# Second product of the first tile half in float32, half in float16 parts, and magnitudes and soft-max high parts of two batches on ScalarE

## The chip, the core and the metric

The kernel runs on one core of a Trainium2 chip. Five engines work side by side, each through its own queue in order: TensorE (PE in the profile; its weight loads are PEld), VectorE (DVE), ScalarE (ACT), GpSimd (POOL) and SyncE (SP), which issues the DMAs here. The metric is the device time of one execution in microseconds (us); less is better.

## The reference

Attention with a sliding window of 128 and a linear bias, then an MLP with Gelu, over 8 batches of 8 heads, 576 positions and 64 per head (4608 tokens, model width 512, inner width 2048):

```python
scores = scale * np.matmul(q, k.transpose(0, 1, 3, 2))
mask = (rel >= 0) & (rel < window)
scores = np.where(mask, scores + bias[None], -1000000000.0)
attn = softmax(scores)
x = concat_heads(np.matmul(attn, v))        # 4608 x 512
h = x @ w_in                                # 512 -> 2048
g = 0.5 * h * (1.0 + erf(h * inv_sqrt2))
out = g @ w_out                             # 2048 -> 512
```

All inputs and the output are float32.

## The kernel before, in words

**Precision.** A float32 matrix is mostly carried as two float16 parts: a high part (the scaled value rounded) and a low part (the scaled value less the high part, line 145). A product is then three float16 matmuls: high by high, high by low, low by high. The scales are powers of two taken from the largest magnitude. Batch 0 of attention (`EXACT = 1`) and the second product of the first tile are done in float32 instead (lines 389 and 619), for which no parts are needed.

**Tiles and stages.** The MLP goes over 9 tiles of 512 tokens. A tile's first product (`mlp_in`, L584) has 16 chunks of 128 inner columns; each is 12 float16 matmuls into one PSUM bank of tag "mm" (four banks), and ScalarE's Gelu empties it (L597 for tile 0, L600 for the others). For tile 0, Gelu writes float32 `g` at once. For the others it writes float32, GpSimd makes the high part (L601) and VectorE the low one. The second product (`mlp_out`) adds all 16 chunks into one bank for each of four blocks of 128 tokens; tile 0 takes the float32 weights `zo` (L619), the others the weight parts `wo` (L622).

**Attention.** One unit is two heads of one batch; a batch has four. `scores` (L399) fills banks of tag "att", VectorE scales them and adds the bias (L421), `softmax` takes the maximum (L491, VectorE), the exponential (L494, ScalarE), the reciprocal of the sum (L498), the high part `e_main` (L500, GpSimd) and the low part (VectorE, L145); a transposing DMA on SP's queue turns them into `et`, and `weigh` (L540) multiplies by v. ScalarE and VectorE cut the result into the parts of `x`, the MLP's input. While tile t is in the MLP, batch t + 1 goes through attention, at steps written out by hand. Tile t takes part of its tokens from batch t and batch t + 1 begins inside it, so a tile needs `weigh` of all four units of batch t before its first product can end.

**q, k and v.** `split_qk` takes the largest magnitude of q and of k (`absmax`, L213, VectorE), spreads it over partitions, and writes the high parts (L356, ScalarE) and the low ones (VectorE) to `qbuf` and `kbuf`, which exist once. `stat_v` and `split_v` do the same for v.

**Weights.** `w_in` and `w_out` come in a packed form and are turned into float32 by two operations of ScalarE (L186, L188) and three of VectorE (L191, L192, L195). Four buffers of tag "wo" hold the float32 `w_out`; its parts need a common scale (`weights_out_scale`), and then take the places of the float32 weights one after the other. Two of the eight pairs of parts go to a buffer of tag "ld", which q and k of batch 2 need next, and are copied from there by a DMA (`wo_first`, L278) when the last "wo" buffer is free.

**Order.** The kernel is written with a framework that keeps all dependencies and plans the order of each engine's queue: it takes the order of the text as priorities (`tc.high_priority` raises some) and issues by modelled times. Buffers are given by tag when a free one of the tag is there. So the text after line 680 (the loop over weight pairs `n` with tile 0's first product, then the loop over `m` with its second product and the units of batch 1, then the tiles) is a wish and the trace shows what came of it.

## Time and profile before

| what | value |
|---|---|
| median of 3 runs | 958.84 us (958.63 to 960.74) |
| profiled execution | 957.65 us, span 955.8 us |
| busy share of the span | PE 96%, DVE 66%, ACT 47%, POOL 27% |
| granted TensorE clock, mean | 0.988 |
| tile 0: first product | about 66 to 111 us |
| tile 0: second product, with batch 1's units | 111.4 to 188.1 us |
| tile 1's first matmul | 187.9 us |
| one steady tile (393.5 to 491.6 us) | 98 us |

The profile has one page (busy shares, 40 equal slices of the span with digits for tenths of busy time, the chain of waits that ended last, the costliest groups) and a trace that answers further questions. In a timeline a row is: start, time, engine, line, operation, tiles (written <- read), shape, count, and in brackets how long the engine had been idle before and what released it. In a table by stage a row gives, for each engine, its busy time and its number of instructions.

### The profile page before, as it was taken

How to read it: one execution, taken by the hardware profiler on the slowest of the kernel's cores; microseconds unless marked ns; L12 is line 12 of the kernel's file. 1: busy time of each engine (PE TensorE's matmuls, PEld its weight loads, DVE VectorE, ACT ScalarE, POOL GpSimd, SP SyncE). 2: the span in 40 equal slices, each digit the busy share in tenths (PEclk: the TensorE clock that was granted, in tenths of full speed). 3: DMA queues.
4: the chain of work that ended last, by engine and by line, in shares of the span. 5: the costliest groups of instructions: out<-in, count | busy, mean ns of one | idle time of the engine just before them, and what ended most of it. 6: DMA issues, size and time to landing. Idle time of an engine off the chain costs nothing.

```text
span 955.8 us, 17566 instructions
## 1 busy us (share of the span) xinstructions
PE 920.2 (96%) x7036; PEld 450.0 (47%) x7036; DVE 634.8 (66%) x1254; ACT 449.5 (47%) x957; POOL 253.5 (27%) x516
## 2 busy tenths in 40 slices
PE   6979999899798999999999999999999999999998
PEld 3554444444454445444544445444544454444443
DVE  6899989769886978588767876777566722201200
ACT  5977556344563665256626643664366313101200
POOL 1010004323441533144313530353044312201200
PEclk8999999899999999999999999999999999999999
DMA  9527615762367424713371346245312430000000
GB/s 324 199 96 244 222 50 74 132 188 100 72 135 166 76 51 106 193 32 66 79 193 45 66 95 171 56 79 95 73 28 51 86 81 1 1 23 23 0 12 34
DMA packets 172451, 91.18 MB, mean 95 GB/s; under 512 B 132561, under 2 KB 153169, under 8 KB 172241
## 3 DMA queue, kind: packets, MB, share of 16 engines
q1 hardware_dynamic: 172368, 90.06, 38.3%
q8 instruction: 55, 0.90, 0.4%
q14 instruction: 28, 0.22, 0.1%
HBM read 46.53 MB, written 9.44 MB: 59 GB/s over the span
## 4 chain that ended last, share of the span: by engine, by line
PE 68%; DVE 8%; ACT 4%; DMA 3%; issue 2%; POOL 1%; SPq 0%; POOLq 0%; ACTq 0%; DVEq 0%
PE o L622 31%; PE h L584 29%; PE av L540 4%; PE sc L399 3%; DMA et<-e_main 2%; ACT s L494 2%; DVE e_main L145 2%; DVE s L421 1%; DVE g L145 1%; DVE nmax L491 1%; DVE stq L213 1%; POOL e_main L500 1%; DMA q<-qp 1%; DVE wo L145 1%; DMA v<-vp 1%
## 5 line engine op out<-in xcount | busy, mean ns | idle before, releaser
L584 PE MATMUL h<-x,wi 128*128 128x512 f16 x1728 | 381.8, 379 | 5.0 <-ACT g L600 3.3
L584 PEld LDWEIGHTS <-wi 128*128 128x128 f16 x1728 | 166.2, 98 | 205.8 <-issue 7.3
L622 PE MATMUL o<-wo,g 128*128 128x512 f16 x1152 | 260.2, 380 | 0.0
L622 PEld LDWEIGHTS <-g 128*128 128x128 f16 x1536 | 145.9, 98 | 175.2 <-issue 0.7
L601 POOL TENSOR_SCALAR g<-g,sg 128x512 f16<-128x512 f32 x128 | 104.2, 818 | 286.1 <-ACT g L600 280.4
L494 ACT ACTIVATE s<-s,nmax 128x192 f32<-128x192 f32 x252 | 111.2, 442 | 121.4 <-DVE nmax L491 114.4
L145 DVE SCALAR_TENSOR_TENSOR g<-g,sg,g 128x512 f16<-128x512 f32 x128 | 106.1, 841 | 90.4 <-POOL g L601 90.3
L500 POOL TENSOR_SCALAR e_main<-s,z 128x192 f16<-128x192 f32 x252 | 121.4, 499 | 126.1 <-issue 43.6
L600 ACT ACTIVATE g<-h,gs 128x512 f32<-128x512 f32 x128 | 86.0, 686 | 135.0 <-PE h L584 108.6
L145 DVE SCALAR_TENSOR_TENSOR e_main<-s,z,e_main 128x192 f16<-128x192 f32 x252 | 111.0, 482 | 15.3 <-POOL e_main L500 14.8
L622 PE MATMUL o<-wo_first,g 128*128 128x512 f16 x384 | 88.3, 379 | 0.0
L399 PE MATMUL sc<-kbuf,qbuf 64*64 64x192 f16 (+1 forms) x1656 | 73.3, 261 | 8.5 <-DMA kbuf<-kp 4.6
L421 DVE SCALAR_TENSOR_TENSOR s<-sc,cs,bias_h 128x384 f32<-128x384 f32 x112 | 63.6, 607 | 12.2 <-PE sc L399 12.0
L553 ACT ACTIVATE x<-av,cx 128x448 f16<-128x448 f32 (+6 forms) x52 | 23.8, 475 | 91.7 <-PE av L540 91.5
L491 DVE TENSOR_REDUCE nmax<-s 128x5 f32<-128x960 f32 (+1 forms) x56 | 58.5, 1044 | 2.7 <-DVE s L421 0.5
L619 PE MATMUL o<-zo,g 128*128 128x512 f32 x128 | 58.1, 606 | 0.0
L540 PE MATMUL av<-et,vbuf 128*64 128x128 f16 (+1 forms) x1680 | 46.0, 215 | 11.9 <-DMA et<-e_main 11.1
L426 POOL MEMSET s<- 64x128 f32 (+1 forms) x112 | 19.1, 171 | 135.1 <-DVE s L421 134.5
L630 ACT ACTIVATE ob<-o,so 128x512 f32<-128x512 f32 x16 | 10.8, 677 | 90.8 <-PE o L622 90.7
L399 PEld LDWEIGHTS <-qbuf 64*64 64x64 f16 x1512 | 36.2, 107 | 36.8 <-issue 33.5
L540 PEld LDWEIGHTS <-vbuf 128*64 128x64 f16 x1680 | 43.0, 114 | 22.2 <-issue 18.4
L632 DVE TENSOR_SCALAR ob<-o,so 128x512 f32<-128x512 f32 x16 | 11.9, 744 | 60.0 <-PE o L622 60.0
(129 smaller groups left out, 737.5 us busy)
## 6 DMA issues: line engine op xcount, KB each, us to landing
v<-vp SPq DMA_DIRECT2D x32, 320.0 KB, 5.2
out<-ob SPq DMA_DIRECT2D x36, 256.0 KB, 2.0
raw<-w_in SPq DMA_DIRECT2D x8, 1024.0 KB, 14.2
raw<-w_out SPq DMA_DIRECT2D x8, 1024.0 KB, 5.0
q<-qp SPq DMA_DIRECT2D x7, 1152.0 KB, 6.1
k<-kp SPq DMA_DIRECT2D x7, 1152.0 KB, 6.0
qbuf<-qp SPq DMA_DIRECT2D x4, 288.0 KB, 4.7
kbuf<-kp SPq DMA_DIRECT2D x4, 288.0 KB, 5.0
```

Of the source, the lines that this page charges most:

```text
L145: nc.vector.scalar_tensor_tensor(out=dst, in0=src, scalar=scale, in1=high, op0=ALU.mult, op1=ALU.subtract)
L399: nc.tensor.matmul(ps[bank][o, n, 0:W], a, m, start=(i == 0), stop=(i == len(terms) - 1 and b > 0), skip_group_check=True,)
L421: nc.vector.scalar_tensor_tensor(out=s[:, bank[0] : bank[0] + k, :], in0=ps[bank][:, 0:k, 0:W], scalar=cs, in1=bias.broadcast_to([P, k, W] ...
L491: nc.vector.tensor_reduce(out=nmax[:, r], in_=s[:, r], axis=AX.X, op=ALU.max, negate=True)
L494: nc.scalar.activation(s[:, i, :], s[:, i, :], AF.Exp, bias=nmax[:, i : i + 1], accum_out=z[:, i : i + 1])
L500: nc.gpsimd.tensor_scalar(e[:, i, 0, c], s[:, i], z[:, i : i + 1], 1.0, op0=ALU.mult, op1=ALU.mult)
L540: nc.tensor.matmul(av[r, (j - blocks[0]) * QB : (j - blocks[0] + len(js)) * QB], v32s[b][:, hp, kb, r] if b < EXACT else vbuf[:, vi, hp, k ...
L584: nc.tensor.matmul(ph, wi[n][:, a, cc, k * P : (k + 1) * P], x[:, cc, b, :], start=(i == 0), stop=(i == 3 * NCC - 1),)
L600: nc.scalar.activation(g32, ph, AF.Gelu, scale=gsc[t, n])
L601: nc.gpsimd.tensor_scalar(g[:, r, 0], g32, gsg[t, n], 1.0, op0=ALU.mult, op1=ALU.mult)
L619: nc.tensor.matmul(o, g[:, r, c], zo[n][:, n % 2, k * DM : (k + 1) * DM], start=(fc == 0), stop=(fc == NFC - 1))
L622: nc.tensor.matmul(o, g[:, r, a, c], wo[n][:, b, k, :], start=(fc == 0 and i == 0), stop=(fc == NFC - 1 and i == 2),)
```

## The change

It edits seven things.

1. Tile 0's second product: token blocks 0 and 1 (`WHOLE = 256` tokens) stay in float32; blocks 2 and 3 take three float16 matmuls with parts of `g` and `wo`. Both kinds of `g` share one buffer: 256 columns of float32, and 256 columns seen as two float16 parts.
2. Tile 0's Gelu is split: 256 columns go to `g`, 256 to a float32 buffer `rest` (tag "ob"), from which ScalarE makes the high part and VectorE the low one.
3. The tile's scales are computed with each pair of weights (`weights_in`) instead of chunk by chunk.
4. `split_qk` of batches 1 and 2 takes the sum of magnitudes on ScalarE (`AF.Abs` with an accumulated sum, writing into `qbuf` and `kbuf`) in place of the maximum on VectorE. The sum is a bound of the maximum, so the scale is smaller.
5. The soft-max high parts of batches 1 and 2 are made by ScalarE instead of GpSimd.
6. `stat_v(1)`, `split_qk(1)`, `split_v(1)` and `load_v(2)` move from pair 3 to pair 7, and a small copy makes the statistics wait for the low part of chunk 8 or 5; `stat_v(2)` moves behind the third step of the second product, and `split_qk(2)` waits for the last sum of batch 1's soft-max.
7. The second product's loop: eight steps in float32, then eight in float16 in the order 2 to 7, 0, 1; the first weight parts are made ahead of it, the others during the float32 steps; scores at steps 1 and 4, `weigh` at 5, 8, 11 and 15.

```diff
+WHOLE = 256
...
         inverse(sww[:, r], pww[:, r])
+        tile_scales(0, ns)
...
-    def split_qk(b):
+    def split_qk(b, gate=None):
         q32, k32 = qk32.pop(b)
         stat = small([P, 2], f"stq{b}", 2, tag="stq")
-        absmax(stat[:, 0:1], q32)
-        absmax(stat[:, 1:2], k32)
+        if gate is not None:
+            nc.vector.tensor_copy(stat, gate.broadcast_to([P, 2]))
+        for n, (src, buf) in enumerate(((q32, qbuf), (k32, kbuf[:, :, PAD:]))):
+            if b < 3:
+
+                nc.scalar.activation(buf[:, 0], src, AF.Abs, accum_out=stat[:, n : n + 1])
+            else:
+                absmax(stat[:, n : n + 1], src)
...
+                if st.b < 3:
+                    nc.scalar.activation(e[:, i, 0, c], s[:, i], AF.Copy, scale=z[:, i : i + 1])
+                    continue
                 nc.gpsimd.tensor_scalar(e[:, i, 0, c], s[:, i], z[:, i : i + 1], 1.0, op0=ALU.mult, op1=ALU.mult)
...
         if t == 0:
-            nc.scalar.activation(g[:, r], ph, AF.Gelu, scale=gsc[t, n])
+            nc.scalar.activation(g[:, r, 0:WHOLE], ph[:, 0:WHOLE], AF.Gelu, scale=gsc[t, n])
+            if k == 0:
+                rests[n] = pool.tile([P, 2, TT - WHOLE], F32, tag="ob", name=f"g32_{t}_{n}", bufs=3)
+            rest = rests[n][:, k]
+            nc.scalar.activation(rest, ph[:, WHOLE:TT], AF.Gelu, scale=gsc[t, n])
+            hi, lo = (halves_of(g, r)[:, a] for a in range(2))
+            nc.scalar.activation(hi, rest, AF.Copy, scale=gsg[t, n])
+            low_part(lo, rest, gsg[t, n], hi)
             return
...
+    def halves_of(g, r):
+
+        return g[:, r, WHOLE:TT].bitcast(F16).rearrange("p (a s) -> p a s", a=2)
+
+    def low_of_first(fc):
+
+        return halves_of(g_of[0, fc // 4], fc % 4)[:, 1, 0:1]
...
+        whole = t == 0 and tb * P < WHOLE
...
-        if t == 0:
-            nc.tensor.matmul(o, g[:, r, c], zo[n][:, n % 2, k * DM : (k + 1) * DM], start=(fc == 0), stop=(fc == NFC - 1))
+        if whole:
+            nc.tensor.matmul(o, g[:, r, c], zo[n][:, n % 2, k * DM : (k + 1) * DM], start=(fc == first), stop=(fc == last))
         else:
+            if t == 0:
+                both, c = halves_of(g, r), slice(tb * P - WHOLE, (tb + 1) * P - WHOLE)
+            else:
+                both = g[:, r]
             for i, (a, b) in enumerate(((0, 0), (0, 1), (1, 0))):
                 nc.tensor.matmul(
-                    o, g[:, r, a, c], wo[n][:, b, k, :],
-                    start=(fc == 0 and i == 0), stop=(fc == NFC - 1 and i == 2),
+                    o, both[:, a, c], wo[n][:, b, k, :],
+                    start=(fc == first and i == 0), stop=(fc == last and i == 2),
                 )
...
-            tile_scales(0, [n])
             for k in range(2):
                 mlp_in(0, 2 * n + k)
-        if n == 3:
-            stat_v(1)
-            split_qk(1)
+        weights_out_raw(n)
+        if n == 7:
+            stat_v(1, low_of_first(8))
+            split_qk(1, low_of_first(5))
             split_v(1)
             load_v(2)
-        if n == 5:
-            stat_v(2)
-        weights_out_raw(n)
         fetch(1)
...
-    scores_at, weigh_at, split_at = {1: 2, 3: 3}, {2: 0, 4: 1, 6: 2}, {5: 0, 6: 2, 7: 4}
-    for m in range(NWP):
+    out_scale(0)
+    weights_out_split(0)
...
+    whole = range(WHOLE // P)
+    todo = [(m, whole, 0, NFC - 1) for m in range(NWP)]
+    order = list(range(2, NWP)) + [0, 1]
+    todo += [(m, range(WHOLE // P, NTB), 2 * order[0], 2 * order[-1] + 1) for m in order]
+    scores_at, weigh_at, split_at = {1: 2, 4: 3}, {5: 0, 8: 1, 11: 2, 15: 3}, {1: 2, 3: 4, 5: 6}
+    for n, (m, tbs, first, last) in enumerate(todo):
         for fc in (2 * m, 2 * m + 1):
-            for tb in range(NTB):
-                mlp_out(0, tb, fc)
-        if m in scores_at:
-            all_scores(unit(1, scores_at[m]))
-            softmax(unit(1, scores_at[m]))
-        if m in weigh_at:
-            weigh(unit(1, weigh_at[m]))
-        if m in split_at:
-            weights_out_split(split_at[m])
-    weigh(unit(1, 3))
-    weights_out_split(6)
+            for tb in tbs:
+                mlp_out(0, tb, fc, first, last)
+        if n in split_at:
+            weights_out_split(split_at[n])
+        if n == 2:
+            stat_v(2)
+        if n in scores_at:
+            all_scores(unit(1, scores_at[n]))
+            softmax(unit(1, scores_at[n]))
+        if n in weigh_at:
+            weigh(unit(1, weigh_at[n]))
     load_qk(2)
-    split_qk(2)
+    split_qk(2, unit(1, 3).z[:, NG - 1 : NG])
```

More of the change, by code (lines that the diff above doesn't have):

```diff
@@ L304, in load_v, with stat_v @@
         v32s[b] = v32
-    def stat_v(b):
+    def stat_v(b, gate=None):
         stat = small([P, 1], f"stv{b}", 2, tag="stv")
+        if gate is not None:
+            nc.vector.tensor_copy(stat, gate)
         absmax(stat, v32s[b].rearrange("p h n d -> p (h n d)"))
@@ L343, in load_qk @@
         qk32[b] = (q32.rearrange("p h s -> p (h s)"), k32.rearrange("p h s -> p (h s)"))
-    def split_qk(b):
+    def split_qk(b, gate=None):
         q32, k32 = qk32.pop(b)
         stat = small([P, 2], f"stq{b}", 2, tag="stq")
-        absmax(stat[:, 0:1], q32)
-        absmax(stat[:, 1:2], k32)
+        if gate is not None:
+            nc.vector.tensor_copy(stat, gate.broadcast_to([P, 2]))
[4 more added lines that the diff above has]
+                absmax(stat[:, n : n + 1], src)
         pw, sc = pow2(f"q{b}", stat, 2, 2, b < 2)
@@ L564, in tile_scales @@
         r = slice(ns[0], ns[-1] + 1)
-        big = k > 1
-        gs = small([P, k], f"gs{t}_{ns[0]}", 2, tag=f"gs{int(big)}")
+        gs = small([P, k], f"gs{t}_{ns[0]}", 4 if t == 0 else 2, tag=f"gs{k}")
         nc.vector.tensor_scalar(gs, pww[:, r], pwx[t], 2.0 ** -26, op0=ALU.mult, op1=ALU.mult)
-        if t == 0:
-            for n in ns:
-                gsc[t, n] = gs[:, n - ns[0] : n - ns[0] + 1]
-            return
-        sg = small([P, k], f"sg{t}_{ns[0]}", 2, tag=f"sg{int(big)}")
+        sg = small([P, k], f"sg{t}_{ns[0]}", 4 if t == 0 else 2, tag=f"sg{k}")
         nc.vector.tensor_scalar(sg, sww[:, r], sx[t], 2.0 ** -22, op0=ALU.mult, op1=ALU.mult)
@@ L575, in tile_scales @@
             gsc[t, n], gsg[t, n] = gs[:, n - ns[0] : n - ns[0] + 1], sg[:, n - ns[0] : n - ns[0] + 1]
+    rests = {}
     def mlp_in(t, fc):
@@ L610, in attention_gelu_mlp, with mlp_out @@
     o_ps = {}
-    def mlp_out(t, tb, fc):
+    def mlp_out(t, tb, fc, first=0, last=NFC - 1):
         n, k = divmod(fc, 2)
-        if fc == 0:
+        whole = t == 0 and tb * P < WHOLE
+        if fc == first:
             o_ps[t, tb] = psum.tile([P, DM], F32, tag="mm", name=f"o{t}_{tb}", bufs=4)
@@ L617, in mlp_out @@
         c = slice(tb * P, (tb + 1) * P)
-        if t == 0:
-            nc.tensor.matmul(o, g[:, r, c], zo[n][:, n % 2, k * DM : (k + 1) * DM], start=(fc == 0), stop=(fc == NFC - 1))
-        else:
+        if whole:
+            nc.tensor.matmul(o, g[:, r, c], zo[n][:, n % 2, k * DM : (k + 1) * DM], start=(fc == first), stop=(fc == last))
+        else:
+            if t == 0:
+                both, c = halves_of(g, r), slice(tb * P - WHOLE, (tb + 1) * P - WHOLE)
+            else:
+                both = g[:, r]
             for i, (a, b) in enumerate(((0, 0), (0, 1), (1, 0))):
                 nc.tensor.matmul(
-                    o, g[:, r, a, c], wo[n][:, b, k, :],
-                    start=(fc == 0 and i == 0), stop=(fc == NFC - 1 and i == 2),
+                    o, both[:, a, c], wo[n][:, b, k, :],
+                    start=(fc == first and i == 0), stop=(fc == last and i == 2),
                 )
-        if fc == NFC - 1:
+        if fc == last:
             ob = pool.tile([P, DM], F32, tag="ob", name=f"ob{t}_{tb}", bufs=3)
-            so_t = so[t] if t else 1.0
+            so_t = 1.0 if whole else so[t]
             if tb % 2:
```

## The prediction

> **What bounds the kernel now.** I read the page's busy table first, then the 40 slices, then busy time by stage, then the timelines of PE and DVE in the stages that the change touches.
>
> ```profile
> span 955.8 us, 17566 instructions
> PE 920.2 (96%) x7036; PEld 450.0 (47%) x7036; DVE 634.8 (66%) x1254; ACT 449.5 (47%) x957; POOL 253.5 (27%) x516
> ...
> PE   6979999899798999999999999999999999999998
> ...
> DVE  6899989769886978588767876777566722201200
> ```
>
> PE is busy for 96% of the span, so what can be won is matmul time (920.2 us) or the 35.6 us in which PE is idle. The slices say where the idle time lies: from slice 14 (about 335 us) on PE reads 9 throughout. DVE is high in the first quarter and falls to 5 to 7 later. So the change, which works on the stage from about 60 to 310 us, meets a stretch in which PE and DVE are both near full. The busy time by stage (engines PE, PEld, DVE, ACT, POOL, then granted clock, DMA share, GB/s):
>
> ```profile
> 60.00:190.00 130.00, 122.93 (x826) 62.46 (x823) 120.17 (x214) 73.64 (x140) 22.49 (x56) 0.96 0.57 149
> 190.00:310.00 120.00, 110.32 (x948) 54.73 (x947) 93.19 (x176) 54.02 (x114) 38.95 (x71) 0.99 0.52 131
> 310.00:400.00 90.00, 90.00 (x812) 43.84 (x812) 71.60 (x147) 47.98 (x108) 32.00 (x66) 1.00 0.46 101
> ```
>
> Tile 0 (60 to 190) leaves PE 7.1 us idle and DVE 9.8. Tile 1 (190 to 310) leaves PE 9.7 and DVE 26.8. After that PE has no idle time, so a microsecond by which tile 2 starts earlier is a microsecond of the whole. The chain of waits, which runs on PE in its last 170 us, says the same; its last row is one half of a tile, and it also gives the price of a float16 matmul: 192 in 41.45 us, 0.216 us each.
>
> ```profile
> 910.61 41.45 PE o L622 x192
> ```
>
> **PE work removed.** The timeline of PE, first for the two products of tile 0, then for its end and for the waits of tile 1:
>
> ```profile
> 80.33 31.24 PE L584 MATMUL h<-x,wi 128*128 128x512 f16 x144 [1.24 <-ACT g L597]
> 111.40 20.76 PE L619 MATMUL o<-zo,g 128*128 128x512 f32 x48
> 132.10 1.42 PE L399 MATMUL sc<-kbuf,qbuf 64*64 64x192 f16 x42
> 174.81 1.60 PE L540 MATMUL av<-et,vbuf 128*64 128x128 f16 x66
> 180.82 2.77 PE L540 MATMUL av<-et,vbuf 128*64 128x128 f16 x66 [4.42 <-DMA et<-e_main]
> 183.53 4.55 PE L619 MATMUL o<-zo,g 128*128 128x512 f32 x8
> 187.92 7.93 PE L584 MATMUL h<-x,wi 128*128 128x512 f16 x36
> 195.78 1.60 PE L540 MATMUL av<-et,vbuf 128*64 128x128 f16 x66
> 197.72 2.75 PE L584 MATMUL h<-x,wi 128*128 128x512 f16 x12 [0.35 <-ACT x L553]
> 225.70 0.68 PE L399 MATMUL sc<-kbuf,qbuf 64*64 64x192 f16 x16
> 241.93 0.27 PE L399 MATMUL sc<-kbuf,qbuf 64*64 64x192 f16 x2 [0.58 <-DVE s L421]
> 259.83 2.32 PE L540 MATMUL av<-et,vbuf 128*64 128x128 f16 x54 [4.08 <-DMA et<-e_main]
> 299.52 1.55 PE L540 MATMUL av<-et,vbuf 128*64 128x128 f16 x54 [2.60 <-DMA et<-e_main]
> ```
>
> A float32 product of the second layer is two records of the trace: 16 chunks by 4 token blocks are 64 calls, and L619 has 128 records. So 48 records are 24 products, and 20.76 / 24 = 0.865 us each. Half of the calls, 32, become three float16 matmuls: 3 x 0.216 = 0.648 us. PE loses 32 x (0.865 - 0.648) = 7.0 us. The whole second product falls from 55.4 to 27.7 + 20.7 = 48.4 us. That is certain as work; whether it is time hangs on what else holds the end of tile 0.
>
> **What holds the end of tile 0.** In DVE's timeline batch 1's last soft-max block comes late (the first two rows are for later):
>
> ```profile
> 101.95 2.57 DVE L213 TENSOR_REDUCE stq<-k 128x1 f32<-128x2304 f32 x1
> 165.57 2.46 DVE L145 SCALAR_TENSOR_TENSOR wo<-zo,s,wo 128x1024 f16<-128x1024 f32 x2
> 179.89 1.93 DVE L145 SCALAR_TENSOR_TENSOR e_main<-s,z,e_main 128x192 f16<-128x192 f32 x4
> 185.54 0.69 DVE L632 TENSOR_SCALAR ob<-o 128x512 f32<-128x512 f32 x1 [3.32 <-PE o L619]
> 187.87 1.42 DVE L145 SCALAR_TENSOR_TENSOR e_main<-s,z,e_main 128x192 f16<-128x192 f32 x4
> ```
>
> It ends at 187.87 + 1.42 = 189.3, its transposing DMA lets the last attention product start at 195.78, and only after it is the input of tile 1 whole (197.72). With 48.4 us of second product, PE would have done its work by 111.4 + 48.4 + 8.4 (scores) + 4.8 (three attention products of 1.6) = 173.0, and the 36 matmuls of tile 1 that it can do ahead (36 x 0.216 = 7.8 us) by 181. The 8.4 us stand in the first row of the next fence. DVE, not PE, then sets this end, so DVE's work is summed. Groups of 60 to 190 us (busy us, mean ns of one):
>
> ```profile
> L399 PE MATMUL sc<-kbuf,qbuf 64*64 64x192 f16 x216 | 8.4, 246 | 0.5 <-DVE s L421 0.5
> L213 DVE TENSOR_REDUCE stq<-q 128x1 f32<-128x2304 f32 x2 | 5.1, 2543 | 0.0
> L213 DVE TENSOR_REDUCE stq<-k 128x1 f32<-128x2304 f32 x1 | 2.6, 2570 | 0.0
> L145 DVE SCALAR_TENSOR_TENSOR x<-tail,sx,x 128x256 f16<-128x256 f32 x1 | 0.5, 479 | 0.0
> L145 DVE SCALAR_TENSOR_TENSOR e_main<-s,z,e_main 128x192 f16<-128x192 f32 x36 | 15.7, 480 | 1.0 <-POOL e_main L500 0.8
> ```
>
> - Removed: three maxima over q and k go to ScalarE, 5.1 + 2.6 = 7.7 us.
> - Added: 16 low parts of 128x256, as `x<-tail`, 16 x 0.479 = 7.7 us. The tile scales keep their number (8 instructions before, 4 + 4 after), and the two copies that serve as gates are of 128x1 and 128x2.
> - The low parts of the weights of attention: the four at 179.89 run beside POOL and take 0.48 us each, the four at 187.87 mostly without it, 0.36. Taking POOL off these 36 is worth between 0 and 36 x 0.12 = 4.4 us; I take half, 2.2.
> - The 3.32 us that DVE waits for `o` go, because that product ends some 10 us earlier for PE.
>
> In the Trainium skill, "GPSIMD Engine Reference", section "8. Key points", POOL shares its SBUF interfaces with VectorE and contends with VectorE instructions that have two SBUF inputs, as these low parts have. By that rule the whole 4.4 us would come back and the forecast would be 2.2 us lower; the two rows agree in direction.
>
> So the last soft-max ends 2.2 + 3.3 = 5.5 us earlier, at about 184, and tile 1's input is whole 5.5 us earlier. PE then waits some 9 us there, in place of the 4.42 us at 180.82; what follows such a wait runs slow for a while (66 matmuls in 2.77 us against 1.60, eight float32 records in 4.55 against 8 x 0.432 = 3.46), and I leave that as it is now, 2.3 us.
>
> **ScalarE's new work** lies beside this. Its rows:
>
> ```profile
> 79.59 2.42 ACT L597 ACTIVATE g<-h,gs 128x512 f32<-128x512 f32 x4
> 141.08 0.45 ACT L494 ACTIVATE s<-s,nmax 128x192 f32<-128x192 f32 x1 [2.79 <-DVE nmax L491]
> L512 ACT ACTIVATE x<-tail,sx 128x256 f16<-128x256 f32 x1 | 0.5, 510 | 0.0
> L356 ACT ACTIVATE qbuf<-q,scq 128x2304 f16<-128x2304 f32 x1 | 2.2, 2201 | 0.0
> L186 ACT ACTIVATE zo<-raw 128x1024 f32<-128x1024 f32 x8 | 9.4, 1170 | 14.5 <-DMA raw<-w_out 14.5
> ```
>
> A Gelu of 128x512 (2.42 / 4 = 0.605 us) becomes two Gelus of half the width and a scaled copy. Each of the three lies between the 0.45 of a 128x192 and the 0.51 of the one 128x256; I take 0.48, nearer the row of the same size: 16 x (3 x 0.48 - 0.605) = 13 us. The sums of magnitudes of q and k are 2 x 2.2 for batch 1 and as much for batch 2. The high parts are 36 x 0.45 = 16 us for each of batches 1 and 2. Up to 190 us ScalarE goes from 73.6 to about 73.6 + 13 + 4.4 + 4.4 + 16 = 111 of 130 us. I cost this at nothing on PE, because the first product has four banks of 2.6 us (12 x 0.216) each before a late Gelu stops it, and behind that product ScalarE has 19 us free before 190. If the cover is gone, a Gelu queued behind a conversion that waits for `raw` (14.5 us over eight of them) delays PE; between 0 and 13 us, and DVE's soft-max, which sets the end, would hide most of it. The new gates hold nothing of DVE: counted on from 80.33, where four chunks are done, PE ends chunk 5 at 85.5 and chunk 8 at 93.3, so their low parts are due by about 87 and 95, while k of batch 1 was reduced only at 102. The statistics and loads of v that move behind them are not due before tile 1.
>
> **Tile 1.** Its waits are 0.58 + 4.08 + 2.60 = 7.3 us, all behind scores and soft-max of batch 2, which begin at 225.70, 38 us after tile 1's first matmul (187.92).
>
> ```profile
> 224.21 2.61 DVE L145 SCALAR_TENSOR_TENSOR kbuf<-k,scq,kbuf 128x2304 f16<-128x2304 f32 x1
> L278 SPq DMA_DIRECT2D wo_first<-wo x1: 542/542/542, 192.9 to 192.9; - x1
> ```
>
> They waited for the parts of q and k, done at 226.8; k's buffer is free only after the copy of the first weight parts (issued on SP's queue at 192.9), which needs the last float32 weight buffer. After the change that buffer is read out 27.7 us of float32 products after 111.4, so the copy can go some 25 us earlier and the scores come at their place, 8 chunks or 21 us after the tile's start instead of 38. DVE loses the maximum over k of batch 2 (2.5) and POOL's neighbourhood once more, and has 26.8 us free. I take 5.5 of the 7.3 us as won; bounds 0 and 7.3 + 0.8 (the slow 2.32 against 1.55 behind the wait).
>
> **The sum.** 5.5 + 5.5 = 11.0 us off the profiled execution of 957.65 (span 955.8 and 1.85 around it): 946.65. The median of the runs shown, 958.84, is 1.2 above it: 947.8.
>
> **Rivals.** *PE sets the end of tile 0 after all.* The scores of batch 1 can start earlier than 132 (two maxima, 5.1 us, no longer stand on DVE ahead of them), and if DVE's idle 9.8 us close up, the attention products wait for nothing. Then the 7.0 us of PE work count in full, with 4.42 + 0.35 and the 2.3 slow us, and all 8.1 of tile 1: 22 us. With half of those waits kept, some 15 to 17 us: 942, at best 937. Against: DVE was 92% busy in this stage (120.17 of 130). Chance 0.2.
>
> *DVE gives nothing back.* The order of issue is planned from modelled times, so the text's new order need not come out as written; the gained idle time reappears as other waits on DVE's in-order queue, now behind ScalarE's high parts, and tile 1's waits stay. Only 0 to 4 us remain: 957. Chance 0.2.
>
> *The weight parts end last (slower).* The float16 half needs all eight weight parts in tile 0; before, the last of them were done at 168 and none was used before tile 1's second product. The last pair stands behind batch 1's last soft-max in the text. If its two low parts (2.46 us) run after 184, they end at 186.5; the copy of the first pair waits for the buffer that they read (0.54 to issue, 5.2 to land: 192.2), then 24 matmuls (5.2) and an eviction (0.7): 198.1. Two of the four banks are held so long, so only 18 instead of 36 matmuls of tile 1 are done by then (3.9 us lost). Tile 1 goes on 0.4 + 3.9 = 4.3 us later than now, with its waits as they are: 963; with a few of them won, 959. It decides from the point where the last low part ends later than 182. Against it: DVE's idle 9.8 us leave room for them earlier. Chance 0.15.
>
> **How the numbers follow.** Forecast 0.45 (6 to 14 us won; 944.8 to 952.8), rivals 0.2, 0.2 and 0.15. Changes within 0.2% (1.9 us), about what a measurement of this kernel can tell from none, are taken from the second rival. Faster 0.45 + 0.2 + 0.12 = 0.77, same 0.08, slower 0.15. The range takes in the forecast, nearly all of the first rival and the second, and leaves out the slower one: 937 to 958.5.
>
> **What would show it.** In the changed profile: 64 records of L619's float32 form and 96 more of the float16 one; PE's busy time near 913; the first product of tile 0 without waits for `g`; batch 1's last low part near 184; the scores of batch 2 about 21 us after tile 1's start; no wait of 4 us in tile 1. I am wrong if PE's first product of tile 0 runs later than 113, if PE waits for `wo` in the float16 half, or if DVE's idle time in tile 0 grows.

## The result

The changed kernel takes 954.13 us (median of 5 runs, 952.48 to 956.14) against 958.84 (5 runs, 958.59 to 962.07): ratio 0.9949, 95% interval 0.9925 to 0.9973. That is 4.7 us faster where 11 were forecast. Run again with the experiments, it took 951.66 against 958.65: ratio 0.993 (0.991 to 0.9949). So the change wins 5 to 7 us.

The page of the changed kernel (span; busy time and share of PE, PEld, DVE, ACT, POOL; the slices of PE and DVE):

```profile
span 954.3 us, 17680 instructions
...
PE 920.4 (96%) x7068; PEld 448.8 (47%) x7068; DVE 626.1 (66%) x1270; ACT 493.4 (52%) x1071; POOL 214.5 (22%) x444
...
PE   7979999889999899999999999999999999999998
...
DVE  6799989689786877497768876777566722201200
```

GpSimd lost 39 us, ScalarE gained 44, VectorE lost 9. PE's busy time is that of before (920.2), not the 913 that were forecast. A second profile of each kernel was taken with the experiments: e14 is the change again, with 913.0 us of PE, and e8 is the kernel before again.

**Where the time went.** The stage that the change touches, cut at the end of tile 1's first product. The columns of these tables by stage are the window, its length, then the busy time of PE, PEld, DVE, ACT, POOL, the granted clock, DMA share and GB/s. Before:

```profile
111.40:234.80 123.40, 115.81 (x843) 56.93 (x843) 102.91 (x203) 58.66 (x119) 34.48 (x68) 0.97 0.47 114
234.80:294.30 59.50, 54.59 (x531) 28.28 (x532) 51.72 (x112) 27.18 (x84) 22.93 (x54) 0.97 0.56 115
```

After:

```profile
114.00:237.30 123.30, 113.33 (x913) 56.95 (x914) 108.45 (x241) 88.97 (x196) 16.49 (x36) 0.96 0.50 121
237.30:288.40 51.10, 51.10 (x493) 25.45 (x494) 41.49 (x78) 31.11 (x92) 3.74 (x14) 1.00 0.63 141
```

The first stretch, from tile 0's second product to the end of tile 1's first, is as long as before: PE is busy 2.5 us less in it (38 records of work, scores above all, moved into it from the second) and idle 2.4 us more (10.0 against 7.6). The second stretch, tile 1's second product, is 8.4 us shorter: 3.5 us of its PE work moved ahead, and 4.9 us of idle time are gone. Since work moved across this cut, a cut at one event is clearer: the start of batch 1's last attention product, which the forecast wanted earlier. All numbers are us, from two profiles of each kernel:

| stretch | before | before again (e8) | change | change again (e14) |
|---|---|---|---|---|
| second product's start to the last attention product of batch 1 | 84.4 | 82.9 | 82.9 | 83.8 |
| PE busy and idle in it | 79.0, 5.4 | 79.4, 3.4 | 74.3, 8.5 | 74.6, 9.2 |
| from there to tile 2's start | 98.5 | 98.5 | 91.5 | 90.9 |
| PE busy and idle in it | 91.4, 7.1 | 91.4, 7.1 | 90.1, 1.5 | 90.1, 0.8 |

Up to that event PE has less to do, and waits as much longer. Behind it, in tile 1, 7.0 to 7.6 us are won, nearly all of it idle time. So the whole gain came in tile 1, and nothing came in tile 0, where half of it was forecast.

**Which waits went and which came.** PE's groups in the whole stage (busy us, mean ns of one, then idle time ahead of the group and what ended it). Before:

```profile
L584 PE MATMUL h<-x,wi 128*128 128x512 f16 x194 | 43.2, 379 | 2.2 <-ACT g L600 1.8 <-ACT x L553 0.3
L399 PE MATMUL sc<-kbuf,qbuf 64*64 64x192 f16 x432 | 16.7, 253 | 1.3 <-DVE s L421 1.3
L540 PE MATMUL av<-et,vbuf 128*64 128x128 f16 (+1 forms) x426 | 13.0, 227 | 9.0 <-DMA et<-e_main 8.5 <-DVE e_main L145 0.5
```

After:

```profile
L595 PE MATMUL h<-x,wi 128*128 128x512 f16 x194 | 43.7, 379 | 2.4 <-ACT ob L661 2.1 <-ACT x L567 0.2
L653 PE MATMUL o<-wo_first,g 128*128 128x512 f16 x72 | 17.5, 394 | 2.8 <-DMA wo_first<-wo 2.8
L410 PE MATMUL sc<-kbuf,qbuf 64*64 64x192 f16 x432 | 17.2, 250 | 2.7 <-DVE s L432 1.5 <-ACT kbuf L367 0.6 <-DVE kbuf L146 0.5
L554 PE MATMUL av<-et,vbuf 128*64 128x128 f16 (+1 forms) x426 | 13.4, 231 | 1.9 <-DMA et<-e_main 1.9
```

The attention products wait 7.1 us less. New are the copy of the first weight parts (2.8), an eviction on ScalarE (2.1) and 1.4 more ahead of the scores. PE's timeline after (start, time, ...) shows their places:

```profile
82.97 31.24 PE L595 MATMUL h<-x,wi 128*128 128x512 f16 x144 [1.11 <-ACT g L612]
114.04 13.90 PE L646 MATMUL o<-zo,g 128*128 128x512 f32 x32
...
170.46 0.59 PE L653 MATMUL o<-wo_first,g 128*128 128x512 f16 x1 [2.77 <-DMA wo_first<-wo]
...
172.07 2.77 PE L554 MATMUL av<-et,vbuf 128*64 128x128 f16 x66
175.84 2.77 PE L554 MATMUL av<-et,vbuf 128*64 128x128 f16 x66 [1.00 <-DMA et<-e_main]
178.54 5.85 PE L653 MATMUL o<-wo_first,g 128*128 128x512 f16 x23
184.23 2.75 PE L595 MATMUL h<-x,wi 128*128 128x512 f16 x12
...
191.97 4.04 PE L595 MATMUL h<-x,wi 128*128 128x512 f16 x18 [2.06 <-ACT ob L661]
196.89 1.60 PE L554 MATMUL av<-et,vbuf 128*64 128x128 f16 x66 [0.88 <-DMA et<-e_main]
199.13 0.28 PE L410 MATMUL sc<-kbuf,qbuf 64*64 64x192 f16 x4 [0.64 <-ACT kbuf L367]
...
320.32 4.89 PE L595 MATMUL h<-x,wi 128*128 128x512 f16 x15 [2.42 <-ACT g L618]
```

Tile 1 begins at 184.23, 3.7 us earlier than before, but the last attention product of batch 1, without which its first product can't end, begins at 196.89 (before: 195.78). The last row is a wait in tile 2. It stands in the place of the 2.60 us at 299.52 before, which the forecast counted to tile 1, though tile 2 had begun at 294.16; the second profiles have the same two waits (2.30 and 2.21).

That tile 1 no longer waits has the reason that was forecast. The copy of the first weight parts, which k's buffer had to wait for, was issued at 192.89 before (81.5 us after the second product's start) and is now issued 50.5 us after it:

```profile
164.55 0.54 SPq L280 DMA_DIRECT2D wo_first<-wo  x1
```

VectorE's timeline tells why batch 1's last soft-max is late:

```profile
136.39 2.82 DVE L214 TENSOR_REDUCE stv<-v 128x1 f32<-128x2560 f32 x1 [2.51 <-DMA v<-vp]
139.13 0.16 DVE L508 TENSOR_SCALAR z<-z 128x5 f32<-128x5 f32 x1
...
163.21 1.27 DVE L146 SCALAR_TENSOR_TENSOR wo<-zo,s,wo 128x1024 f16<-128x1024 f32 x1
...
190.00 0.67 DVE L116 COPY quarters<-stq 32x2 f32<-32x2 f32 x4 [3.17 <-ACT kbuf L358]
...
191.63 0.72 DVE L146 SCALAR_TENSOR_TENSOR e_main<-s,z,e_main 128x192 f16<-128x192 f32 x2
```

And ScalarE's, with one row of SyncE's queue:

```profile
172.89 1.84 ACT L512 ACTIVATE e_main<-s,z 128x192 f16<-128x192 f32 x5 [2.02 <-DMA et<-e_main]
...
176.30 7.38 SPq L517 DMA_TRANSPOSE et<-e_main  x2
...
183.91 1.84 ACT L512 ACTIVATE e_main<-s,z 128x192 f16<-128x192 f32 x5 [2.32 <-DMA et<-e_main]
185.66 2.11 ACT L358 ACTIVATE qbuf<-q 128x2304 f16<-128x2304 f32 x1
...
187.76 2.11 ACT L358 ACTIVATE kbuf<-k 128x2304 f16<-128x2304 f32 x1
...
189.87 1.48 ACT L512 ACTIVATE e_main<-s,z 128x192 f16<-128x192 f32 x4
191.25 0.67 ACT L661 ACTIVATE ob<-o,so 128x512 f32<-128x512 f32 x1
```

The maximum over v of batch 2 stops VectorE's queue for 2.51 us until v has landed, and stands there for 2.82, ahead of a soft-max of batch 1 (L508). The weight part that frees the buffer for the copy comes at 163.21. At the end the two passes over q and k of batch 2 stand on ScalarE ahead of the last four high parts and an eviction, and VectorE's step on their result (190.00) stands ahead of the last four low parts. One more link is in these rows: `e_main`, which holds the parts of a unit's soft-max, exists once, so the high parts of the next unit wait until the transposing DMAs have read it, 2.02 and 2.32 us here (4.3 together in both profiles of the change; before, GpSimd waited 4.1 us so). The last low part ends at 192.35, 78.3 us after the second product's start (78.6 in the second profile); before it was 189.29, 77.9 after (76.4 in the second). That is the step on which the forecast was built.

### The profile page after: what moved, and what is told of

Its sections match the earlier page's. It is cut to its first block, busy times and chain, and to the rows that moved or that the text cites. A ratio compares the mean times of both kernels' runs of the same rounds, so it can differ in the third digit from the quotient of the medians.

```text
span 954.3 us, 17680 instructions
## 1 busy us (share of the span) xinstructions
PE 920.4 (96%) x7068; PEld 448.8 (47%) x7068; DVE 626.1 (66%) x1270; ACT 493.4 (52%) x1071; POOL 214.5 (22%) x444
## 4 chain that ended last, share of the span: by engine, by line
PE 54%; DMA 2%; DVE 2%; ACT 2%; issue 1%; SPq 0%; POOL 0%; DVEq 0%
PE o L653 26%; PE h L595 22%; PE av L554 3%; PE sc L410 2%; DMA v<-vp 1%; DMA q<-qp 1%; DVE stv L214 1%; DMA et<-e_main 1%; ACT vbuf L332 1%; DVE vbuf L146 0%; ACT s L505 0%; DVE kbuf L146 0%; ACT L618 0%; ACT L505 0%; SPq L305 0%
## 5 line engine op out<-in xcount | busy, mean ns | idle before, releaser
L653 PE MATMUL o<-wo,g 128*128 128x512 f16 x1224 | 276.4, 379 | 0.2 <-DVE wo L146 0.2
L653 PEld LDWEIGHTS <-g 128*128 128x128 f16 x1632 | 155.0, 98 | 186.6 <-issue 2.3
L146 DVE SCALAR_TENSOR_TENSOR g<-g,sg,g 128x512 f16<-128x512 f32 (+1 forms) x144 | 114.1, 805 | 92.7 <-POOL g L619 91.5
L619 POOL TENSOR_SCALAR g<-g,sg 128x512 f16<-128x512 f32 x128 | 100.4, 788 | 316.7 <-ACT g L618 312.4
L146 DVE SCALAR_TENSOR_TENSOR e_main<-s,z,e_main 128x192 f16<-128x192 f32 x252 | 107.3, 468 | 15.0 <-POOL e_main L514 10.2
L514 POOL TENSOR_SCALAR e_main<-s,z 128x192 f16<-128x192 f32 x180 | 87.1, 503 | 84.9 <-ACT s L505 29.3
L653 PE MATMUL o<-wo_first,g 128*128 128x512 f16 x408 | 94.6, 382 | 2.8 <-DMA wo_first<-wo 2.8
L410 PE MATMUL sc<-kbuf,qbuf 64*64 64x192 f16 (+1 forms) x1656 | 75.6, 264 | 10.8 <-DMA kbuf<-kp 4.5
L567 ACT ACTIVATE x<-av,cx 128x448 f16<-128x448 f32 (+6 forms) x52 | 23.7, 474 | 72.8 <-PE av L554 72.6
L505 ACT ACTIVATION_READ_ACCUMULATOR s<-s,nmax 128x1 f32 x252 | 47.1, 187 | 0.0
```

The source lines that it names most:

```text
L146: nc.vector.scalar_tensor_tensor(out=dst, in0=src, scalar=scale, in1=high, op0=ALU.mult, op1=ALU.subtract)
L410: nc.tensor.matmul(ps[bank][o, n, 0:W], a, m, start=(i == 0), stop=(i == len(terms) - 1 and b > 0), skip_group_check=True,)
L505: nc.scalar.activation(s[:, i, :], s[:, i, :], AF.Exp, bias=nmax[:, i : i + 1], accum_out=z[:, i : i + 1])
L514: nc.gpsimd.tensor_scalar(e[:, i, 0, c], s[:, i], z[:, i : i + 1], 1.0, op0=ALU.mult, op1=ALU.mult)
L567: nc.scalar.activation(x[:, 0], av[:, :n], AF.Copy, scale=c)
L619: nc.gpsimd.tensor_scalar(g[:, r, 0], g32, gsg[t, n], 1.0, op0=ALU.mult, op1=ALU.mult)
```

## The experiments

Theory: tile 0 gave nothing back because steps that were moved and costed at nothing stand on in-order queues ahead of batch 1's soft-max. Three are candidates: ScalarE's passes and high parts, the copy of the first weight parts, the statistics of v on VectorE. The rivals: PE's work did not really fall, the time was lost elsewhere (before the stage or after it), or the parts of the change work against each other. Medians, and ratios to the kernel before beside it on the same chip:

| label | us | ratio (95%) |
|---|---|---|
| e1_max2_on_dve | 954.77 | 0.9959 (0.9946 to 0.9973) |
| e2_first_parts_in_place | 953.84 | 0.995 (0.9931 to 0.9969) |
| e3_both | 955.85 | 0.9977 (0.9962 to 0.9991) |
| e4_high_on_gpsimd | 955.35 | 0.9966 (0.9949 to 0.9984) |
| e5_v_behind_softmax | 953.45 | 0.9952 (0.9935 to 0.9969) |
| e6_v_behind_in_place | 950.46 | 0.9921 (0.9897 to 0.9946) |
| e7_all_float32 | 962.88 | 1.0036 (1.0018 to 1.0054) |
| e8_before_again | 956.3 | one execution |
| e9_half_alone | 962.7 | 1.0044 (1.0026 to 1.0063) |
| e10_in_place_max2 | 952.13 | 0.9946 (0.9927 to 0.9965) |
| e11_scales_by_chunk | 964.99 | one execution |
| e12_qk_behind_x | 965.13 | 1.0078 (1.0054 to 1.0102) |
| e13_abs_behind_low | 953.18 | 0.9939 (0.9919 to 0.9959) |
| e14_after_again | 951.66 | 0.993 (0.991 to 0.9949) |
| e15_best_again | 947.88 | 0.9888 (0.987 to 0.9906) |

### ScalarE's moved work, and the copied weight parts

Batch 2's magnitudes go back to VectorE's maxima (e1):

```diff
-            if b < 3:
+            if b < 2:
                 nc.scalar.activation(buf[:, 0], src, AF.Abs, accum_out=stat[:, n : n + 1])
```

> The changed kernel with the magnitudes of batch 2 taken on VectorE again (two maxima of 2.5 us) instead of two passes of 2.1 us on ScalarE. Theory A (in the changed kernel the two passes stand on ScalarE's queue ahead of the high parts of batch 1's last soft-max block and of the eviction of tile 0's output, and hold the end of tile 0): the last low part of batch 1 ends 3 to 4 us earlier, the 2.06 us in which PE waited for the eviction go, and the time falls by 2 to 4 us against the changed kernel, to 950 to 952. Theory B (the weight parts hold tile 0): no change beyond 1 us. Theory C (VectorE as a whole holds tile 0): slower by up to 5 us, since VectorE gets 5 us more.

The float16 half reads the first weight parts where they are made, without waiting for the copy (e2), and both together (e3):

```diff
+                parts = held[0][:, n] if n < 2 else wo[n]
...
-                    o, both[:, a, c], wo[n][:, b, k, :],
+                    o, both[:, a, c], parts[:, b, k, :],
...
-    order = list(range(2, NWP)) + [0, 1]
+    order = list(range(NWP))
```

> The changed kernel with the first weight parts of tile 0's float16 half read where they were made, in the order 0 to 7, so that tile 0 does not wait for their copy. Theory B: the wait of 2.77 us for the copy and the slow matmuls after it (some 3 us) go, and the time falls by 3 to 5 us, to 949 to 951. Theory A: the wait goes but PE waits as much more for batch 1's last attention product, and the time stays within 1.5 us of 954.

> Both edits, maxima of batch 2 on VectorE and first weight parts in place. Theory A and B together: 5 to 8 us less than the changed kernel, 946 to 949, with PE waiting less than 2 us between the start of tile 0's second product and tile 1's. Theory C: within 2 us of 954.

The soft-max high parts go back to GpSimd (e4: `if st.b < 3` becomes `if st.b < 0`):

> The changed kernel with the soft-max high parts of batches 1 and 2 on GpSimd again, as before the change. If moving them to ScalarE was worth something by itself (VectorE's low parts run at 0.36 instead of 0.48 us without GpSimd beside them): 3 to 8 us slower than the changed kernel, 957 to 962. If ScalarE's queue is what holds tile 0 (theory A): as fast or up to 3 us faster, 951 to 954.

None of the four is faster than the change by more than 0.3 us, and none of the medians is more than 2 us from its first one (954.13). Against its second measurement, on another chip (ratio 0.993), e1, e3 and e4 are 3 to 4.5 us slower. In e2 PE no longer waits for the copy, but the attention products wait 8.3 us, as long as before. So the copy alone holds nothing, and neither do ScalarE's passes or high parts one by one: in e1, with the passes on VectorE, VectorE does them (at 182.96 and 185.42) ahead of the same low parts. What e4 does show is the price of GpSimd beside VectorE, as rows of the low parts from 60 to 190 us in e4 and then in the second profile of the change:

```profile
L146 DVE SCALAR_TENSOR_TENSOR e_main<-s,z,e_main 128x192 f16<-128x192 f32 x35 | 14.7, 468 | 4.1 <-POOL e_main L514 4.1
```

```profile
L146 DVE SCALAR_TENSOR_TENSOR e_main<-s,z,e_main 128x192 f16<-128x192 f32 x36 | 13.1, 406 | 3.9 <-ACT e_main L512 3.8
```

36 x (0.468 - 0.406) = 2.2 us for batch 1. VectorE's idle time ahead of them stayed the same (4.1 and 3.9), with ScalarE in GpSimd's place.

### The statistics of v

`stat_v(2)` waits for the reciprocal of batch 1's second soft-max instead of coming in front of it (e5), and e5 with e2 (e6):

```diff
-            stat_v(2)
+            stat_v(2, unit(1, 1).z[:, NG - 1 : NG])
```

> The changed kernel with the statistics of v of batch 2 held back by a small copy until the second soft-max block of batch 1 has its sums, so that VectorE's queue does not stand waiting for that load (2.5 us and 2.8 us of reduction) while the first soft-max block of batch 1 waits behind it. Theory D (the chain of batch 1's four soft-max blocks sets the end of tile 0, PE and weight parts do not, and the wait for v stands in that chain): batch 1's first transposing DMA starts 4 to 5 us earlier, tile 1's first product ends 2 to 5 us earlier counted from tile 0's second product, and the time falls to 949 to 952. If that chain has slack: no change beyond 1.5 us.

> The same, with the first weight parts of tile 0's float16 half read where they were made. Theory D: with the chain shorter, the copy's wait of PE is next, so that this is 1 to 3 us faster than the kernel with the statistics held back alone, 947 to 951. If PE's work in tile 0 never sets the end: within 1 us of that kernel.

In e5 VectorE takes v at 164.44 without waiting, and the copy lands in time, so that PE's wait for it is gone too; but ScalarE now has the two passes ahead of all nine high parts of the last soft-max, and the last attention product still waits (3.63 us). In e6 the planned order puts five of the nine ahead. Its last low part ends 75.1 us after the second product's start (e5 76.9, e2 79.1, the change 78.3), and the stretch from there to the end of tile 1's first product is 119.9 us (122.5, 126.1, 123.3). Its median is the best so far, though its interval overlaps that of the change. To see whether that was chance, it ran again beside the change:

> The changed kernel once more. If the 2 us by which its second product began later (114.0 against 111.4 and 113.0) are chance of an execution, the product begins between 111 and 115 here, and the time is 952 to 956 whatever it is; the waits for the copied weight parts and for the eviction in tile 0 should be there again, 2 to 3 us each, since the order of instructions is the same.

> Both edits once more, beside the changed kernel on the same chip. If the two waits hid behind one another, so that only both edits together win, the median is 2 to 5 us below that of the changed kernel. If the 950.46 was chance, the two are within 1 us.

Again it is 3.8 us less (947.88 against 951.66), on one chip and with intervals that do not overlap. In e14 the waits for the copy and the eviction are there again (2.62 and 2.26 us). The last low part of e15 comes 76.5 us after the start, where e6, the same program, had 75.1; so much two profiles of one program differ here. The tables of e15, by stage and by group:

```profile
112.84:285.30 172.46, 161.86 (x1404) 79.44 (x1403) 150.12 (x319) 119.86 (x288) 20.23 (x49) 0.99 0.55 128
```

```profile
L595 PE MATMUL h<-x,wi 128*128 128x512 f16 x194 | 45.5, 389 | 5.2 <-ACT x L567 3.7 <-DVE pwv L134 1.4
...
L554 PE MATMUL av<-et,vbuf 128*64 128x128 f16 (+1 forms) x426 | 11.2, 210 | 3.6 <-DMA et<-e_main 2.1 <-DVE s L432 1.5
```

10.6 us of waits are still there; the largest, 3.35 us, is for parts of x that ScalarE makes behind the two passes. Three edits aim at these. e10 is e6 with the passes back on VectorE (the edit of e1); e12 is e6 with them held until the last part of x, e13 is e6 with them held only until the last low part of the soft-max:

```diff
-    split_qk(2, unit(1, 3).z[:, NG - 1 : NG])
+    split_qk(2, x_tile(1)[:, NPAIR - 1, 1, TT - 1 : TT])
```

```diff
-    split_qk(2, unit(1, 3).z[:, NG - 1 : NG])
+    split_qk(2, e_main[:, NG - 1, 1, 255:256])
```

> The kernel with the statistics of v held back and the first weight parts in place (950.5), with the maxima of batch 2 on VectorE. Theory A, now that the two other waits are gone: the two passes on ScalarE stand before the last soft-max block, and this is 2 to 4 us faster, 946 to 949. If they cost nothing even now: within 1.5 us of 950.5, or slower by VectorE's 5 us of maxima, up to 954.

> The kernel with the statistics of v held back and the first weight parts in place (950.5), with the magnitudes of q and k of batch 2 held back until tile 1's input is whole, so that neither ScalarE nor VectorE has their parts ahead of it. If they hold the end of tile 0 (theory A): PE's wait of 3.4 us for x at 189 goes and the time is 947 to 949. If tile 1 then waits for batch 2 as before the change: 951 to 955.

> The version with both edits (v's statistics behind batch 1's second soft-max, first weight parts read in place) has PE waiting 3.36 us at 188.83 for the parts of x, which ScalarE makes behind two passes of magnitudes over q and k of batch 2 (182.55 to 186.87) and four high parts. Here those passes wait for the last low part of batch 1's soft-max, so that they stand behind its high parts. If the passes in front of the last block are what still holds the end of tile 0, the last attention product of batch 1 begins near 190 instead of 194.04, tile 1's first product ends 2 to 4 us earlier, and the parts of q and k come 4 to 8 us later; with tile 1 still without waits, the median is near 947. If they are not, the last attention product stays within 1 us of 194; and if batch 2's scores then come too late, waits of 3 to 6 us return in tile 1's second product and the median is 951 to 954.

None of the three beats e6. With the passes on VectorE (e10) the median is 1.7 us higher, with intervals that overlap. e12 came 10 us above even the worse of its two cases. Its last low part ends early, 70.1 us after the start, but batch 2's parts come late, and waits of 4.46 us (for a Gelu behind the passes) and 4.04 us (for batch 2's `et`) are in tile 1. PE is idle 17.6 us in the stage (e15: 10.6) and busy 169.0 (161.9) with the same instructions, at a granted clock of 0.95 (0.99). e13 is the clearest. VectorE's low parts, PE, and SyncE's queue:

```profile
182.94 3.04 DVE L146 SCALAR_TENSOR_TENSOR e_main<-s,z,e_main 128x192 f16<-128x192 f32 x9
```

```profile
193.19 2.77 PE L554 MATMUL av<-et,vbuf 128*64 128x128 f16 x66 [6.40 <-DMA et<-e_main]
...
202.82 0.41 PE L410 MATMUL sc<-kbuf,qbuf 64*64 64x192 f16 x8 [1.58 <-ACT kbuf L367]
204.82 7.93 PE L595 MATMUL h<-x,wi 128*128 128x512 f16 x36 [1.60 <-ACT g L618]
```

```profile
184.73 6.23 SPq L517 DMA_TRANSPOSE et<-e_main  x2
```

The last low part ends at 185.98, 70.3 us after the second product's start (115.72), 8 us earlier than in the change and earlier than the 72.6 of the forecast (184 less 111.4). Yet the last attention product begins only 5.4 us earlier (77.5 against 82.9), since the two transposing DMAs hold SyncE's queue until 190.96, and tile 1's first product ends no earlier (123.1 us after the start): PE waits for batch 2's parts and a Gelu instead. So even where the soft-max ended as forecast, the end of tile 0 followed it in part only, and the time did not follow at all. No run gave `e_main` a second buffer or the transposing DMAs another place, so what that link alone costs is open.

### The parts of the change by themselves

Without the float16 half and with all else (e7, whose edit also puts back the whole Gelu of tile 0 and the places of batch 1's units), and the float16 half with its order and gates but none of the work moved to ScalarE (e9):

```diff
-WHOLE = 256
+WHOLE = 512
...
-    scores_at, weigh_at, split_at = {1: 2, 4: 3}, {5: 0, 8: 1, 11: 2, 15: 3}, {1: 2, 3: 4, 5: 6}
+    scores_at, weigh_at, split_at = {0: 2, 2: 3}, {2: 0, 4: 1, 5: 2, 7: 3}, {1: 2, 3: 4, 5: 6}
```

```diff
-            if b < 3:
+            if b < 0:
                 nc.scalar.activation(buf[:, 0], src, AF.Abs, accum_out=stat[:, n : n + 1])
...
-                if st.b < 3:
+                if st.b < 0:
                     nc.scalar.activation(e[:, i, 0, c], s[:, i], AF.Copy, scale=z[:, i : i + 1])
```

> The changed kernel with all of tile 0's second product in float32 (no split Gelu, no parts of it; PE has 7.0 us more work there, ScalarE and VectorE 13 and 7 us less), everything else kept and the units of batch 1 placed at the same times. Theory D: the 7 us of PE work are hidden by batch 1's chain, and the time stays within 2 us of the changed kernel, 952 to 956, or is lower as ScalarE and VectorE have less to do. If the float16 half is what won: 958 to 961.

> The changed kernel with the high parts of the soft-max on GpSimd and the maxima of q and k on VectorE for all batches, so that of the change the float16 half with its new order and gates is left. Theory E (the 7 us of PE work count nearly in full; what was moved to ScalarE is worth nothing): within 2 us of the changed kernel, 952 to 956. If the moves to ScalarE pay for VectorE's new low parts (the forecast's sum of VectorE): 957 to 961.

Each is slower than the kernel before, by 3.5 us (0.0036 x 958.84) and 4.2; together they win 5 to 7. Two rows of e7, then three of e9:

```profile
L647 PE MATMUL o<-zo,g 128*128 128x512 f32 x128 | 57.1, 599 | 0.1
L595 PE MATMUL h<-x,wi 128*128 128x512 f16 x193 | 45.5, 393 | 6.9 <-ACT g L619 6.9
```

```profile
115.80:301.20 185.40, 168.66 (x1404) 82.17 (x1403) 163.96 (x330) 91.24 (x210) 59.70 (x122) 0.94 0.52 120
```

```profile
L653 PE MATMUL o<-wo,g 128*128 128x512 f16 x216 | 53.0, 403 | 5.7 <-DVE wo L146 5.7
...
L554 PE MATMUL av<-et,vbuf 128*64 128x128 f16 (+1 forms) x426 | 13.0, 227 | 9.1 <-DMA et<-e_main 9.1
```

In e7 the float32 calls are back (57.1 us) and ScalarE's Gelus of tile 1 are late: the pass over k of batch 2 stands ahead of them at 200.12, where it has waited 5.24 us for k to land. Batch 1's last low part ends early here too, 66.0 us after the second product's start, and again the tile is not earlier. The stage is as long as before (182.7 us against 182.9 and 181.4); the 3.5 us lie in a later start (115.3) and behind the stage, and one profile can't tell these from chance. In e9 VectorE is busy 164.0 us in the stage against 149.9 in the change, and PE waits 5.7 us for weight parts and 9.1 for `et`: this is close to the third rival of the prediction, weight parts that end last, and the kernel is 4.2 us slower than before. Part of VectorE's 14 us is in its low parts of the soft-max, in e9 and then in the change:

```profile
L146 DVE SCALAR_TENSOR_TENSOR e_main<-s,z,e_main 128x192 f16<-128x192 f32 x72 | 32.1, 498 | 6.2 <-POOL e_main L514 6.2
```

```profile
L146 DVE SCALAR_TENSOR_TENSOR e_main<-s,z,e_main 128x192 f16<-128x192 f32 x72 | 27.1, 423 | 4.7 <-ACT e_main L512 4.5
```

5.0 us go with GpSimd working beside VectorE; the maxima over q and k of one more batch (5.1) and over v of another (2.8) are most of the rest. The moves to ScalarE are what keeps this away; with the rest of the change but without the half they won nothing (e7).

### The start, and the place of the scales

The second product began at 111.4 before and at 114.04 after. e8 is the kernel before once more; e11 computes tile 0's scales chunk by chunk again, as before:

```diff
-        tile_scales(0, ns)
...
+            tile_scales(0, [n])
             for k in range(2):
                 mlp_in(0, 2 * n + k)
```

> The kernel before once more, for a second profile of it. In five profiles of the changed kernel and its variants tile 0's second product starts at 113.7 to 114.6 us, in the one of the kernel before at 111.4, with the same instructions ahead of it. If that is the phase of the clock gate at the start and chance: it starts anywhere from 111 to 115 here. If the change caused it: 111 to 111.8.

> The changed kernel with tile 0's scales made chunk by chunk as before the change, the only part of the change whose instructions lie ahead of the first product of tile 0. If these instructions delay the start: tile 0's first product ends at 111.5 to 113 us, as in the two profiles of the kernel before. If not: 113.7 to 115.5, as in the other profiles of the changed kernel.

e11 says nothing on the scales: the planner ordered much else anew, PE's first product waited 4.90, 3.11 and 3.10 us, and the span was 963.2. e8 began its second product at 113.0. What settles the question is e14, the same program as the change:

```profile
111.00 13.90 PE L646 MATMUL o<-zo,g 128*128 128x512 f32 x32
```

It began 3.0 us earlier than in the first profile. From tile 3's first matmul to tile 4's it took 98.4 us instead of 100.8 (before: 97.9 and 97.6), and its span was 947.8 instead of 954.3, with the stage itself as long (174.7 and 174.4). So a start 3 us later and a tile 2.4 us longer can be chance of one execution. From two profiles of each kernel the stage is 182.2 us before (182.9 and 181.4) and 174.55 after: 7.6 us won. What lies behind the stage took 661.5 and 660.1 us before, 665.9 and 662.1 after; that it is longer by at least 1 us in these profiles, and why, stays open.

## Why the prediction was right and wrong

**PE's work, 7.0 us: right.** The second product's groups in the stage (`zo`, `wo`, `wo_first`) hold 94.6 us after, 102.0 before; 7.4 us less. PE's busy time in the stage fell by 6.0 and 6.2 us in the two pairs of profiles, that of the whole execution to 913.0 in one profile and not at all in the other (920.4). But the removed work was not time: up to the last attention product PE only waits longer.

**Tile 1, 5.5 us of 7.3: right, and too small.** The copy was issued 31 us earlier after the second product's start, where some 25 were forecast, and the scores of batch 2 come at 199.13, where the forecast's rule (21 us after the tile's start) gives 205. From the last attention product to tile 2 7.0 and 7.6 us were won. Not all of it is what the forecast listed: its third wait, 2.60 us, lay in tile 2 and was replaced by one of 2.42, while waits that it did not count in this sum (0.35 for x, 1.82 for a Gelu) shrank or went. No run tested this term by itself.

**The end of tile 0, 5.5 us: wrong.** This is the step that failed: "So the last soft-max ends 2.2 + 3.3 = 5.5 us earlier, at about 184, and tile 1's input is whole 5.5 us earlier." It ended at 192.35, 78.3 us after the second product's start, against 77.9 before: nothing was won, instead of 5.5. The 2.2 us from GpSimd's absence were there (e4), and VectorE's busy time from 60 to 190 us fell from 120.2 to 117.1. But its idle time there grew, from 9.8 to 12.9 us (13.2 in the second profile), for it now waits for v (2.51) and for ScalarE (1.69, 2.08 and 3.17). The statistics of v were "not due before tile 1" and costed at nothing; they stand for 2.51 + 2.82 us on VectorE's queue in front of batch 1's soft-max. e5 alone moved them and brought the last low part 1.4 us forward, which is no more than two profiles of one program differ, so their share is not shown. ScalarE's passes, 4.4 us costed at nothing, stand ahead of the last high parts; e13 moved them, on top of e6, and brought the last low part to 70.3 us after the start, from 75.1 and 76.5 in the two profiles without that edit. That share is shown. The forecast summed VectorE's work and left out in which order its queue, and ScalarE's, would take it, and that the high parts wait for the transposing DMAs.

The second rival had this half right: "the gained idle time reappears as other waits on DVE's in-order queue, now behind ScalarE's high parts". Its other half, that tile 1's waits stay, did not come.

**What follows from that end: wrong too.** e13, e12 and e7 show that an earlier soft-max (70.3, 70.1 and 66.0 us after the start) is not an earlier tile: the transposing DMAs on SyncE's queue, batch 2's parts and the Gelus come next. So this 5.5 was not a size but a chain with further links.

**PE waits 9 us at that place, as one wait: wrong in form.** PE is idle for 8.5 and 9.2 us up to the last attention product, but spread over the copy, the eviction, the scores and `et`. That the sum comes so near is luck, since it was forecast for an end 5.5 us earlier; PE's busy time up to there fell by 4.6 and 4.8 us only, since it ran slower behind the waits. The eviction behind ScalarE's passes was on no list.

**The signs of error.** The first product ended at 114.04, past the 113 that was named, but that was chance (111.00). No wait for `wo` in the half beyond 0.2 us, but 2.8 for `wo_first`: the third rival in a small form. VectorE's idle time in tile 0 grew, as said: this sign held. The wait of 4 us in tile 1 is gone.

**The parts add up: not said, and wrong.** The forecast priced each edit beside the kernel before. e7 and e9 show that neither half of the change wins alone.

**The time.** The time came out between the forecast and the second rival: 4.7 us less, and 7.0 when measured again, of 11.0. It rests on the tile 1 term alone.

## What to carry to other kernels

When work is moved to an engine with free time, ask which instruction of the critical chain stands behind it in that queue: a share of 92% or 52% does not tell, and a step that waits for a DMA stops all behind it. After an edit that only removes work from a full engine, follow the chain from there link by link (low part, transposing DMA, attention product, next tile's parts) before its time is counted; here the second link took most of it. Test parts that share an engine together as well as alone: two halves that each lost 4 us won 5 to 7 together, and two profiles of one program differed by 3 us in the start of a product.

## What the runs showed of the hardware

The same instructions take another time in another execution. The first batch's attention in float32, in the first and then in the second profile of the changed kernel:

```profile
31.45 3.95 PE L554 MATMUL av<-et,v 128*64 128x128 f32 x36
```

```profile
30.98 2.13 PE L554 MATMUL av<-et,v 128*64 128x128 f32 x36
```

From 20 to 66 us the granted clock was 0.85 in the one and 0.91 in the other, and tile 0's first matmul came at 69.4 and 65.9. The Trainium skill, "TensorE: Matmul & The Clock Gate", section "Part 1: The HAM clock gate (the "warmup" mystery)", says that the window in which the gate watches PE runs freely, so that the number of slow matmuls varies from run to run of one kernel, and puts the cost below 1% of a span; the two spans, 954.3 and 947.8, differ by 0.7%. That the clock alone makes this difference no run here shows.

Some waits cost PE more than their length: 66 attention matmuls took 2.77 us at 172.07, soon after the wait of 2.77, and 1.60 at 196.89, behind one of 0.88. So that wait cost at least 1.2 us more than its length. Over the stage the same shows in PE's busy time for the same 1404 records: 161.9 us in e15 (granted clock 0.99), 164.4 in the change (0.97) and 169.0 in e12 (0.95).
